# Row selection on TensorE for the first two sub-blocks of a dynamic convolution with a squared-ReLU FFN

## The chip, the core and the metric

The kernel runs on one core of a Trainium2 chip. The metric is the device time of one execution in microseconds, as the median over several runs. The engines named below are TensorE (PE, matmul; PEld is its weight load), VectorE (DVE), ScalarE (ACT), GpSimd (POOL) and SyncE (SP). SP only issues DMAs here, and POOL mostly does.

## The reference

Two layers follow each other over 8 sequences of 4096 rows of 192 features.

The first is a dynamic convolution. Each row has, for each of 8 heads, 7 raw weights. They go through a softmax over the 7 taps, and the row's output is the weighted sum of the row itself and the 6 rows before it, head by head (24 features each):

```python
w = np.exp(weight_gen - max); w = w / (sum + 1e-09)            # (B, S, 8, 7)
x_unf = x_pad[:, np.arange(S)[:, None] + np.arange(7)[None, :], :]
out = np.einsum('bshk,bskhg->bshg', w, x_unf.reshape(B, S, 7, 8, 24))
```

The second is a feed-forward layer on all 32768 rows: `h = max(x @ w_in, 0)`, then `(h * h) @ w_out`, with 2048 hidden features.

## The kernel before, in words

**Sub-blocks and blocks.** The rows are cut into 64 sub-blocks of 512 (`TB`). `BLOCKS` holds two blocks of one sub-block each, then blocks of two sub-blocks. In a block of two sub-blocks, the upper 64 rows of the 128-row array work for one of them and the lower 64 for the other ("half"). The first two blocks cut their one sub-block in two halves of 256 rows in the same way.

**Softmax and rows.** The softmax of sequence 0 is done in four parts of 1024 rows, 8 rows per partition: `exp` on ScalarE (line 250), `total` (257), `recip` (264) and `scale` (272) on VectorE. `scale` writes the weights into `v_first`, whose row order is that of the partitions: partition p holds rows 8p to 8p+7. The convolution needs them one row per partition, in five overlapping tiles of 128 rows per sub-block, `wr`. Before, `wr_load_sbuf` (363) moves them there by DMAs from SBUF to SBUF. The first part feeds sub-blocks 0 and 1; sub-block 0's five DMAs go over SP and POOL, those of sub-block 1 over POOL.

**Band and convolution.** `st_band` (381) multiplies the `wr` tile by `mask` and so spreads the seven weights of each row onto a band matrix `bd`. `st_conv` (487) multiplies x with the band: TensorE matmuls with 32 output features each, on one of four column strips of the array, into `yp`. A copy (503) brings `yp` to `y` in half precision.

**Units and quarters.** A unit, `st_unit` (518), makes 1024 columns of hidden values `h` in PSUM: for each half, the 192 features are contracted in three slots of 64. ScalarE takes the ReLU into `t1` (532), VectorE squares it into `g` (536). `st_mm2` (560) is the second matrix product; one call handles 8 of the 16 hidden chunks for a quarter of 256 rows, and the letter M in the plans stands for one such call. `o_sum` (574, 576) and `o_store` (581) end a quarter after its second call. Since the two halves sit in different rows of the array, `w_i` is kept twice: part 0 as loaded and part 1 with the upper and lower 64 partitions swapped. The swap of half q=0 of `w_i` is done by TensorE with the matrix `swap` (149) and two copies (153), the swap of q=1 by two DMAs (`cross_w_in`, 141).

**Order.** It is written out by hand. Each engine takes its instructions in the order in which the program names them. Before the first unit stands a start-up section with `spin` matmuls (624), which compute nothing that is used. Then each block has a plan: a string whose letters are steps. u is a unit, M a call of `st_mm2`, C the convolution of the next block, E and S the exp and the rest of a softmax part, B the bands of a sub-block, L the load of a part, X the cast of x. M always takes the next call that is due (`quarters`).

**Buffers.** The PSUM pool `ps_h` has three buffers in rotation, shared by `h` and `yp`; `ps_o` has the two banks `o0` and `o1`. `w_out` is loaded by POOL in four pieces (`load_w_out`, 194) after the copy `gate` (657) has seen x of sub-block 1.

Of the kernel before, what the change touches and what calls it, by code (L numbers as in the profile page):

```python
# [9 lines left out]
def kernel(  # L10
# [26 lines left out]
    nc = tc.nc  # L37
    f32 = mybir.dt.float32
# [17 lines left out]
    BLOCKS = [(0, 1), (1, 1)] + [(n, 2) for n in range(2, NSUB, 2)]  # L56
    NBLK = len(BLOCKS)
    NF = Dff // P

# [9 lines left out]
    starts = [BASE + STEP * i for i in range(NT)]  # L69
    bounds = [0, 104, 208, 312, 416, TB]  # L70

    AluOp = mybir.AluOpType
# [24 lines left out]
    mask = const.tile([P, P, 2], f16, name="mask")  # L97
    swap = const.tile([P, P], f16, name="swap")
    FIRST = 8
    PARTS = {0: (8, 8, 8, 8), 1: (8, 8, 16), 2: (16, 16)}  # L100
    v_big = const.tile([P, R + 2 * HALO, HP, SL, 2], f16, name="v_big")
# [3 lines left out]

    def half_swap():

        nc.gpsimd.memset(swap, 0.0)
        for base in (RT, -RT):
            nc.gpsimd.affine_select(  # L110
                out=swap, in_=swap, pattern=[[-1, P]], compare_op=AluOp.not_equal,
                fill=1.0, base=base, channel_multiplier=1,
            )

# [24 lines left out]
    def cross_w_in(q):  # L139
        for r0, r1 in ((0, RT), (RT, 0)):  # L140
            nc.sync.dma_start(out=w_i[r0 : r0 + RT, q, 1], in_=w_i[r1 : r1 + RT, q, 0])

    def cross_w_in_by_pe(q):
        n = NQ + NQ // 2
        for a in range(0, n, 2 * TB):
            b = min(a + 2 * TB, n)
            pt = ps_h.tile([P, 2 * TB], f32, name="pt", tag="h")
            for c in range(a, b, TB):
                nc.tensor.matmul(
                    out=pt[:, c - a : c - a + TB], lhsT=swap, rhs=w_i[:, q, 0, c : c + TB],  # L150
                    start=True, stop=True,
                )
            nc.scalar.copy(out=w_i[:, q, 1, a:b], in_=pt[:, 0 : b - a])

# [145 lines left out]

    x_t, wr_t, bd_t, yp_t, y_t, g_t, gp_t, t1_t, o_t, o_sb_t = ({} for _ in range(10))

# [51 lines left out]
    def wr_load_sbuf(j, parts, order, engines):  # L354
# [3 lines left out]
        for i in order:  # L358
            t0 = max(j % NBB * TB + tile_start(j, i), 0)
            for s in parts:  # L360
                a, b = max(t0, s.t0), min(t0 + P, s.t0 + P * s.r)
                if a < b:
# [6 lines left out]
                    n += 1  # L369

    def st_band(j, tiles):


        if j not in bd_t:
            bd_t[j] = p_bd.tile([P, H * NT * STEP], f16, name="bd")
        i = tiles[0]
        lo = STEP * i
        shift = 0 if i == 0 and j % NBB == 0 else lo - tile_start(j, i)
        n = min(STEP, P - shift)
        shape = (P, HP * len(tiles), n // SL, 2 * SL)  # L380
        nc.vector.tensor_tensor(  # L381
            out=bd_t[j][:, H * lo : H * (lo + len(tiles) * n)].rearrange(
                "p (g m c) -> p g m c", g=shape[1], c=2 * SL
            ),
            in0=wr_t[j][:, i : tiles[-1] + 1]
            .rearrange("p t g c -> p (t g) c")
            .unsqueeze(2)
            .broadcast_to(shape),
            in1=mask[:, shift : shift + n]
            .rearrange("p (m c) e -> p m (c e)", c=SL)  # L390
            .unsqueeze(1)
            .broadcast_to(shape),
            op=AluOp.mult,
        )
# [7 lines left out]
    def conv_pieces(j):  # L402
# [5 lines left out]
        for half in (0, 1):  # L408
# [4 lines left out]
            ])  # L413
        if n == 2:
            for k in range(NK):
                for later in (True, False):
                    for pair in zip(*halves):
                        for s, i, half, a, b, base in pair:
                            for q in (2 * k, 2 * k + 1):
                                yield later, s, i, q, half, a, b, base  # L420
        else:
            for pair in zip(*halves):
                for later in (True, False):
                    for k in range(NK):
                        for s, i, half, a, b, base in pair:
                            for q in (2 * k, 2 * k + 1):
                                yield later, s, i, q, half, a, b, base

# [37 lines left out]
    def st_conv(j):  # L466

        if j >= FIRST_SPREAD:
            return st_conv_spread(j)
        n = BLOCKS[j][1]  # L470
        th = n * TB // 2
        per = 1024 // th
        y = p_y.tile([P, NK, TB], f16, name="y")
        y_t[j] = y
        yps = [
            ps_h.tile([P, 2 * TB], f32, name="yp", tag="h") for _ in range(-(-NK // per))
        ]
        for later, s, i, q, half, a, b, base in conv_pieces(j):
# [6 lines left out]
            k = q // 2  # L485
            col = th * (k % per) - base
            nc.tensor.matmul(  # L487
                out=yps[k // per][p0 : p0 + m, col + a : col + b],
                lhsT=x_t[s][:, i, 32 * q : 32 * q + m],
# [6 lines left out]
        for n, yp in enumerate(yps):  # L496
            k0, k1 = n * per, min((n + 1) * per, NK)

            copies = ((k0, k1, nc.scalar.copy),)
            if j == 0:  # L500
                copies = ((0, 2, nc.scalar.copy), (2, NK, nc.vector.tensor_copy))
            for a, b, copy in copies:
                copy(  # L503
                    out=y[:, a:b, 0:th],
                    in_=yp[:, (a - k0) * th : (b - k0) * th].rearrange("p (k c) -> p k c", c=th),
                )

    def st_unit(j, u):

        th = BLOCKS[j][1] * TB // 2  # L510
        per = TB // th
        w = w_p if j >= FIRST_SPREAD else w_i
        h = ps_h.tile([P, 2, TB], f32, name="h", tag="h")
        for jj in range(per):
            for slot in range(NK):
                for half, r0 in enumerate((0, RT)):
                    k = slot ^ half if slot < 2 else slot
                    nc.tensor.matmul(  # L518
                        out=h[:, half, jj * th : (jj + 1) * th],
                        lhsT=w_in_chunk(w, u * per + jj, slot, half),  # L520
                        rhs=y_t[j][r0 : r0 + RT, k, 0:th],
                        start=(jj == 0 and slot == 0), stop=(slot == NK - 1),
                        skip_group_check=True,
                        tile_position=(r0, 0),
                    )
# [22 lines left out]
    def st_mm2(j, qt, fcs, ccs, o):  # L548


        th = BLOCKS[j][1] * TB // 2
        per = TB // th
        half, off = divmod(qt * QT, th)
        for fc in fcs:
            g = g_t[(j, fc // per)][:, half, fc % per * th + off :]
            for cc in ccs:
# [38 lines left out]
    with nc.allow_low_precision("fp16 matmul pipeline"), tc.manual_schedule():  # L595
# [19 lines left out]
        gate = const.tile([P, 1], f32, name="gate")  # L615
        nc.vector.memset(warm, 0.0)
        for v in v_first:
            nc.vector.memset(v, 0.0)
# [3 lines left out]
        def spin(n):  # L622
# [3 lines left out]
        s0, s1, s2 = parts[:3]  # L626
        spin(25)
        half_swap()
        band_mask()
# [4 lines left out]
            for q in (0, 1)  # L634
        ]
        load_w_in(w_st[0], 0, nc.sync)
        x_load_f32(0)
        load_w_in(w_st[1], 1, nc.sync)
# [3 lines left out]
        s0.scale(0, s0.rh, nc.vector)  # L642
        nc.scalar.copy(out=w_i[:, 0, 0], in_=w_st[0])
        wr_load_sbuf(0, [s0], (0, 2, 1, 4, 3), (nc.sync, nc.gpsimd))
        wr_load_sbuf(1, [s0], range(NT), (nc.gpsimd,))
        x_cast(0, nc.scalar.copy)
        cross_w_in_by_pe(0)
        spin(14)
        x_load_f32(1)
        nc.scalar.copy(out=w_i[:, 1, 0], in_=w_st[1])  # L650
        cross_w_in(1)
        s1.load(nc.sync)
        for i in (0, 2, 1, 3, 4):
            st_band(0, (i,))
        st_conv(0)

        nc.gpsimd.tensor_copy(out=gate, in_=x_st[1][:, 0:1])
        for q in range(4):
# [9 lines left out]
        plans = {  # L668
            0: "B1 X1 u u u E1 S1 u C u u u u",
            1: "L3 u u B2 M E2 B3 u M E2 u u S2 u M u C u S2 M",  # L670
            2: "L4 u u u E3 M u u u M B4 u u u u M B5 S3 u u u u M u E3 C u",
            3: "L5 L6 M S3 u u u M u u u u M u M B6 E4 u u u M M B7 u u u E4 M u M C S4 u",
        }
# [94 lines left out]
        def quarters():  # L768

            for j in range(NBLK - 1):  # L770
                for qt in range(2 * BLOCKS[j][1]):
                    o = new_o(ps_o, 1, qt % 2) if j < 2 else new_o(ps_o)
                    st_mm2(j, qt, FCS[0], (0, 1), o)
                    yield
                    st_mm2(j, qt, FCS[1], (0, 1), o)
                    o_sum(j, qt, (0, 1), o)
                    if qt % 2:
                        o_store(j, qt - 1, range(4), nc.sync)
                    yield

        mm2 = quarters()
        for j in range(NBLK):
            if j + 2 < NBLK:
                load_rows(j + 2)
            u = 0
            for step in plans[j].split():
# [23 lines left out]
                elif kind == "L":  # L810
                    parts[n].load(nc.sync)
                elif kind == "X":
                    x_cast(n, nc.vector.tensor_copy)
# [47 lines left out]
```

The softmax here doesn't subtract the row's maximum and nothing guards it: scores larger than these inputs give would overflow.

## Time and profile before

| | us |
|---|---|
| median of 6 runs | 734.82 (734.37 to 737.21) |
| profiled execution | 734.35 |
| its span | 732.6 |
| TensorE busy in the span | 724.8 (99%) |
| VectorE busy | 627.3 (86%) |
| ScalarE busy | 613.6 (84%) |
| start of the first unit | 15.49 |
| start of the first ReLU | 16.60 |
| start of the convolution of block 2 | 33.33 |
| start of block 2's first unit | 37.05 |

The span runs from the first to the last instruction on the core, and all start times below count from its beginning. TensorE's busy time contains pipelined waits, so 99% says that TensorE always has something to do, not that it works at its peak. The granted TensorE clock is 1.00 in all slices.

### The profile page before, as it was taken

How to read it: one execution, taken by the hardware profiler on the slowest of the kernel's cores; microseconds unless marked ns; L12 is line 12 of the kernel's file. 1: busy time of each engine (PE TensorE's matmuls, PEld its weight loads, DVE VectorE, ACT ScalarE, POOL GpSimd, SP SyncE). 2: the span in 40 equal slices, each digit the busy share in tenths (PEclk: the TensorE clock that was granted, in tenths of full speed). 3: DMA queues.
4: the chain of work that ended last, by engine and by line, in shares of the span. 5: the costliest groups of instructions: out<-in, count | busy, mean ns of one | idle time of the engine just before them, and what ended most of it. 6: DMA issues, size and time to landing. Idle time of an engine off the chain costs nothing.

```text
span 732.6 us, 31124 instructions
## 1 busy us (share of the span) xinstructions
PE 724.8 (99%) x14106; PEld 528.9 (72%) x14106; DVE 627.3 (86%) x856; ACT 613.6 (84%) x724; POOL 99.8 (14%) x148
## 2 busy tenths in 40 slices
PE   8999999999999999999999999999999999999998
PEld 4757777777777777777777777777777777777777
DVE  5999898998898988888988888988889988778753
ACT  5998888988888888888888888888888888888883
POOL 7312222320001100011000010010100110001000
PEclk9999999999999999999999999999999999999999
DMA  8745444783545452455333554334544315444012
GB/s 222 119 96 123 81 71 105 144 160 115 99 66 128 95 90 60 78 125 119 62 73 69 117 123 83 61 71 120 104 87 86 57 49 120 67 87 78 30 45 67
DMA packets 126544, 68.71 MB, mean 94 GB/s; under 512 B 85193, under 2 KB 122636, under 8 KB 125900
## 3 DMA queue, kind: packets, MB, share of 16 engines
q1 hardware_dynamic: 80908, 48.12, 22.9%
q0 software_dynamic: 45360, 18.50, 21.7%
q8 instruction: 110, 1.80, 1.0%
q14 instruction: 22, 0.18, 0.1%
q10 hardware_dynamic: 144, 0.10, 0.0%
HBM read 50.18 MB, written 28.70 MB: 108 GB/s over the span
## 4 chain that ended last, share of the span: by engine, by line
PE 96%; ACT 1%; DMA 1%; DVE 1%; issue 0%; DVEq 0%
PE o L560 47%; PE h L518 45%; PE yp L450 4%; PE yp L487 1%; ACT t L532 1%; DMA wr<-v_first 0%; DMA wg<-in_weight_gen_dram 0%; DVE bd L381 0%; ACT ex L250 0%; DVE v_first L272 0%; ACT y L503 0%; DVE ssum L257 0%; DVE rcp L264 0%; DVE y L503 0%; ACT o_sb L574 0%
## 5 line engine op out<-in xcount | busy, mean ns | idle before, releaser
L532 ACT ACTIVATE t<-h 128x1024 f16<-128x1024 f32 x512 | 496.4, 1026 | 60.0 <-PE h L518 59.7
L560 PEld LDWEIGHTS <-g 64*128 64x128 f16 (+1 forms) x8032 | 342.7, 94 | 55.7 <-issue 2.5
L560 PE MATMUL o<-w_o,g 64*128 64x192 f16 (+1 forms) x8032 | 379.1, 243 | 0.0
L536 DVE TENSOR_TENSOR g<-t 128x2048 f16<-128x2048 f16 (+1 forms) x309 | 309.3, 1037 | 28.1 <-ACT t L532 27.7
L518 PE MATMUL h<-y,w_p 64*128 64x512 f16 x2400 | 291.7, 376 | 0.0
L518 PEld LDWEIGHTS <-w_p 64*128 64x128 f16 x2400 | 113.8, 94 | 94.8
L381 DVE TENSOR_TENSOR bd<-wr,mask 128x4160 f16<-128x4160 f16 (+3 forms) x89 | 149.4, 1703 | 3.5 <-DMA wr<-v_first 3.5
L576 DVE TENSOR_TENSOR o_sb<-o,o_sb 128x384 f32<-128x384 f32 x123 | 68.4, 556 | 60.8 <-ACT o_sb L574 59.9
L333 POOL DMA_DIRECT2D xt<-in_x_dram x62 | 51.8, 839 | 421.6 <-PE yp L450 362.6
L574 ACT COPY o_sb<-o 128x384 f32<-128x384 f32 x129 | 61.5, 477 | 46.8 <-PE o L560 46.0
L518 PE MATMUL h<-y,w_i 64*128 64x512 f16 (+1 forms) x768 | 82.2, 350 | 1.7 <-ACT t L532 0.7
L518 PEld LDWEIGHTS <-w_i 64*128 64x128 f16 x768 | 36.8, 94 | 28.1 <-issue 3.9
L450 PEld LDWEIGHTS <-xt 128*32 128x32 f16 x2000 | 24.5, 95 | 10.6 <-issue 10.6
L272 DVE TENSOR_TENSOR v_big<-ex,rcp 128x112 f16<-128x112 f32 (+5 forms) x180 | 29.8, 236 | 1.9 <-DMA vd<-v_big 0.9
L460 DVE CAST y<-yp 128x1024 f16<-128x1024 f32 x25 | 30.4, 1218 | 0.0
L450 PE MATMUL yp<-bd,xt 128*32 128x104 f16 (+1 forms) x2000 | 28.3, 210 | 0.0
L250 ACT ACTIVATE ex<-wg 128x560 f32<-128x560 f32 (+4 forms) x38 | 25.9, 683 | 1.8 <-DMA wg<-in_weight_gen_dram 1.8
L257 DVE TENSOR_REDUCE ssum<-ex 128x80 f32<-128x560 f32 (+4 forms) x38 | 25.3, 666 | 2.3 <-ACT ex L250 2.3
L460 ACT CAST y<-yp 128x1024 f16<-128x1024 f32 x25 | 25.2, 1007 | 0.0
L264 DVE RECIPROCAL rcp<-ssum 128x80 f32<-128x80 f32 (+4 forms) x38 | 22.8, 601 | 1.3
L323 POOL DMA_DIRECT2D xt<-in_x_dram x7 | 3.9, 555 | 124.6 <-PE yp L450 109.7
L363 POOL DMA_DIRECT2D wr<-v_first x31 | 16.9, 563 | 16.0 <-DVE v_first L272 15.8
(34 smaller groups left out, 95.1 us busy)
## 6 DMA issues: line engine op xcount, KB each, us to landing
out_dram<-o_sb SPq DMA_DIRECT2D x63, 384.0 KB
xt<-in_x_dram POOLq DMA_DIRECT2D x42, 240.0 KB, 5.2
wg<-in_weight_gen_dram SPq DMA_DIRECT2D x4, 1064.0 KB
xt<-in_x_dram POOLq DMA_DIRECT2D x20, 192.0 KB, 4.7
wr<-vd SPq DMA_DIRECT2D x38, 80.0 KB
vd<-v_big SPq DMA_DIRECT2D x5, 512.0 KB
y<-y SPq DMA_DIRECT2D x100, 24.0 KB
wg<-in_weight_gen_dram SPq DMA_DIRECT2D x5, 392.0 KB
```

What stands on the lines that cost most here:

```text
L250: nc.scalar.activation(out=self.ex[:, lo:hi].rearrange("p r g k e -> p (r g) k e"), in_=self.wg[:, lo:hi].rearrange("p r (g e) k -> p (r g ...
L272: eng.tensor_tensor(out=bass.AP(tensor=v.tensor, offset=v.offset + lo * H * SL + lo % SL * 2 + g * SL * 2, ap=[list(v.ap[0]), [H * SL + 2, ...
L333: eng.dma_start(out=dst[:, first:last], in_=ap)
L381: nc.vector.tensor_tensor(out=bd_t[j][:, H * lo : H * (lo + len(tiles) * n)].rearrange("p (g m c) -> p g m c", g=shape[1], c=2 * SL), in0= ...
L450: nc.tensor.matmul(out=yp[p0 : p0 + 32, k - k0, a:b], lhsT=x_t[s][:, i, c0 : c0 + 32], rhs=bd[:, head // 2, e, 0 : b - a], start=True, sto ...
L460: copy(out=y[:, k0 : k0 + 2], in_=yp)
L518: nc.tensor.matmul(out=h[:, half, jj * th : (jj + 1) * th], lhsT=w_in_chunk(w, u * per + jj, slot, half), rhs=y_t[j][r0 : r0 + RT, k, 0:th ...
L532: nc.scalar.activation(out=t1[:, e], in_=h, func=ActF.Relu)
L536: nc.vector.tensor_tensor(out=g[:, a : e + 1], in0=t1[:, a : e + 1], in1=t1[:, a : e + 1], op=AluOp.mult)
L560: nc.tensor.matmul(out=oo[:, cc * Dm : (cc + 1) * Dm], lhsT=g[r0 : r0 + n, cc * P : (cc + 1) * P], rhs=w_o[r0 : r0 + n, fc, :], start=(fc ...
L574: nc.scalar.copy(out=o_sb, in_=o[0][:, c])
L576: nc.vector.tensor_tensor(out=o_sb, in0=o[1][:, c], in1=o_sb, op=AluOp.add)
```

## The change

1. **Rows.** For sub-blocks 0 and 1, TensorE picks the rows. `sel` holds a shifted selection pattern, so that a window of 128 of its columns takes every row of a residue r to its place. Eight accumulating matmuls of 64 columns (r from 0 to 7) make one `wr` tile in PSUM (`pr`), and ScalarE copies it to `wr`. The five tiles of sub-block 0 come first; those of sub-block 1 stand between the five tiles of sub-block 0's convolution. The row DMAs of these two sub-blocks go. `swap` and its selects go; `sel` is cleared by VectorE and filled by one affine select on POOL ahead of `mask`.
2. **First two blocks.** The convolution puts features 0 to 127 on all four column strips, as block k=0 over all 512 columns, and features 128 to 191 twice, on both halves, as k=1. A unit then makes two chunks of hidden features for 512 rows: two matmuls over 128 rows of the array and two over 64 rows, with a change of order from unit to unit. It needs part 0 of `w_i` only.
3. **`w_i`.** Half q=0 is cast by ScalarE between the row copies, half q=1 by VectorE (step W). Both swapped parts are made by DMAs on SP, issued at the start of block 1 (q=0) and of block 2 (q=1).
4. **Order.** x of sub-block 0 is loaded ahead of `w_i`. Block 0's plan makes C before S1, with one unit more before it, and has an M before its last two units; block 3's plan has one M fewer, its first. The calls of the first two blocks come first half of both quarters, then second half of both. 21 spins instead of 25 at the start, and none of the 14 later ones.

The core of the diff:

```diff
-    def half_swap():
...
+    def row_select():
+        nc.gpsimd.affine_select(
+            out=sel, in_=sel, pattern=[[-1, NSEL]], compare_op=AluOp.not_equal,
+            fill=1.0, base=FIRST - 1, channel_multiplier=FIRST,
+        )
...
+    def select_rows(j, s, tiles, places):
...
+            for r in range(s.r):
+                c = a + FIRST - 1 - r
+                nc.tensor.matmul(
+                    out=pr, lhsT=sel[:, c : c + P],
+                    rhs=s.v[:, HALO + r].rearrange("p g c e -> p (g c e)"),
+                    start=(r == 0), stop=(r == s.r - 1),
+                )
...
+    def st_conv_first(j, between=None):
...
+        places = [(q, 32 * q, 0) for q in range(4)]
+        places += [(q, r0 + 32 * (q - 4), 1) for r0 in (0, RT) for q in (4, 5)]
+        for i in ROW_ORDER:
...
+            for later in (True, False):
+                for q, p0, k in places:
...
+            if between:
+                between(i)
+        if j == 0:
+            nc.scalar.copy(out=y[:, 0], in_=yp[:, 0])
+            nc.vector.tensor_copy(out=y[:, 1], in_=yp[:, 1])
...
+    def first_unit(u, h, y):
+        q, f = divmod(u, NF // WQ // 2)
+        both = [
+            (h[:, n], w_i[:, q, 0, (f + n * NF // WQ // 2) * P :][:, 0:P], y[:, 0], 0)
+            for n in (0, 1)
+        ]
+        upper = [
+            (h[:, n], w_i[r0 : r0 + RT, q, 0, NQ + f * P :][:, 0:P], y[r0 : r0 + RT, 1], r0)
+            for n, r0 in enumerate((0, RT))
+        ]
+        pairs = (upper, both) if u % 2 else (both, upper)
...
+        nc.vector.memset(sel, 0.0)
...
-        spin(25)
-        half_swap()
+        spin(21)
+        row_select()
...
+        x_load_f32(0)
         load_w_in(w_st[0], 0, nc.sync)
-        x_load_f32(0)
         load_w_in(w_st[1], 1, nc.sync)
...
-        nc.scalar.copy(out=w_i[:, 0, 0], in_=w_st[0])
-        wr_load_sbuf(0, [s0], (0, 2, 1, 4, 3), (nc.sync, nc.gpsimd))
-        wr_load_sbuf(1, [s0], range(NT), (nc.gpsimd,))
         x_cast(0, nc.scalar.copy)
-        cross_w_in_by_pe(0)
-        spin(14)
         x_load_f32(1)
-        nc.scalar.copy(out=w_i[:, 1, 0], in_=w_st[1])
-        cross_w_in(1)
         s1.load(nc.sync)
+        select_rows(0, s0, ROW_ORDER, (o1, ring, ring, ring, o0))
+        copy_rows(0, ROW_ORDER)
...
+        def next_rows(i):
+            n = ROW_ORDER.index(i)
+            select_rows(1, s0, (i,), ((o1, ring, ring, o0, o1)[n],))
+            if n < 2:
+                copy_rows(1, (i,))
+            if n == 1:
+                nc.scalar.copy(out=w_i[:, 0, 0], in_=w_st[0])
+
+        st_conv_first(0, next_rows)
+        copy_rows(1, ROW_ORDER[2:])
...
-            0: "B1 X1 u u u E1 S1 u C u u u u",
+            0: "B1 X1 W u u u u E1 C S1 u u M u u",
...
-            3: "L5 L6 M S3 u u u M u u u u M u M B6 E4 u u u M M B7 u u u E4 M u M C S4 u",
+            3: "L5 L6 S3 u u u M u u u u M u M B6 E4 u u u M M B7 u u u E4 M u M C S4 u",
...
+            if 1 <= j <= WQ:
+                cross_w_in(j - 1)
...
+                elif kind == "W":
+                    nc.vector.tensor_copy(out=w_i[:, 1, 0], in_=w_st[1])
```

Blocks 1 and 2 keep their plans ("L3 u u B2 M E2 B3 u M E2 u u S2 u M u C u S2 M" and "L4 u u u E3 M u u u M B4 u u u u M B5 S3 u u u u M u E3 C u").

## The prediction, made before the changed kernel was run

> **What bounds it now.** I read the PE waits first, then the chain of work in order of time, then DVE, SP and PE in order of time. After 15 us TensorE waits for other engines only three times, and after 100 us never:
>
> ```profile
> PE h L518 <- ACT t L532: 0.7, 1, 0.7
> PE h L518 <- ACT y L503: 0.7, 1, 0.7
> PE yp L487 <- DVE xt L347: 0.3, 1, 0.3
> ```
>
> So a microsecond won or lost on TensorE before block 4 arrives whole at the end, and the rest is a fixed tail. The chain shows what the change touches (start, length, work):
>
> ```profile
> 6.76 1.47 DVE v_first L272 x8
> 8.25 3.38 DMA wr<-v_first
> 11.72 2.61 DVE bd L381 x5
> 14.38 0.45 PE yp L487 x16
> 14.86 0.59 ACT y L503
> 15.47 0.44 DVE y L503
> 15.95 0.63 PE h L518 x8
> 16.60 2.25 ACT t L532 x3
> ```
>
> The row transfer takes 3.38 us, and the first ReLU starts at 16.60. From there to 28.8 ScalarE runs without a gap at 0.91 us per ReLU, while TensorE has holes: the ACT-bound stretch. VectorE is nearly gapless from 15.8 to 41.7, and two lines of its order and two of SP's will matter:
>
> ```profile
> 15.81 2.35 DVE L381 TENSOR_TENSOR bd<-wr,mask 128x3328 f16<-128x3328 f16 x2
> 39.16 0.72 DVE L272 TENSOR_TENSOR v_first<-ex,rcp 128x84 f16<-128x84 f32 x4
> 12.93 1.16 SPq L141 DMA_DIRECT2D w_i<-w_i  x2
> 39.90 3.67 SPq L363 DMA_DIRECT2D wr<-v_first  x5
> ```
>
> The profiled execution took 734.35 us, span 732.6 and 1.7 around it; the median is 734.82, 0.5 above. I sum against 734.35 and shift the result by 0.5.
>
> **The head.** The load, exp, total, reciprocal and the products stay and end at 8.22. The new memset of `sel` (1031 columns; 640 words take 0.59 us, so at most 1.1) lies in VectorE's 2.31 us idle before `ssum`. The affine select over 1031 columns is not in the trace: 128 columns take 0.29, 256 of the mask 1.24. That bounds it between 1.0 (memset-like rate) and 5.0 us; I take 1 to 2.3, as the 128-column row has the same one-dimensional pattern. The mask is then done by 6.4 to 7.7, before the first band at 8.9; only 5.0 makes it late, by about 1.4.
>
> One tile of rows is 8 matmuls of 64 columns with full 128x128 weights. No row has that. In M the 128x128 pairs start 82.5 ns apart for 192 columns (80 of streaming, 2.5 more): the weight load is hidden. In the conv, matmuls on one column strip start 25 ns apart for 48 columns, 27 for 56, 47 for 104. So 64 columns lie between 27 and 82.5 ns; I take 30, as the first two weight loads of an M start 15 ns apart. A tile: 0.24 us. On one rule I decide against the page: the Trainium skill, TensorE: Matmul & The Clock Gate, Back-to-back issue gap, gives 81 ns for a stream of weight load and matmul at 128 columns, 28 above streaming. M's 2.5 above streaming disagrees; by the page a tile would take about 0.44 and the sum below would end near no change.
>
> First tile: six matmuls remain after the last product, 0.15, then 0.24 from a last conv matmul's start to the ScalarE copy that needs it: 8.64. The copy of 64 columns, from 477 ns at 384 and 1023 at 1024, is 0.20. Band 0 starts at 8.9 and ends at 9.5; five bands 0.50 apart end at 11.5. TensorE finishes the five tiles at 9.4, and then alternates: conv tile (16 matmuls in 4 rounds of 47 ns) 0.19, rows for sub-block 1 0.24, and twice a change of array layout. The layout's price: sixteen M matmuls are 1.32 us, but from M's start at 25.46 to the next unit's at 26.88 it takes 1.43, so 0.1. Together 0.62 per tile, four times: the fifth conv tile starts at 12.0 and its copy at 12.4. ScalarE's cast of `w_i` (1.47, after two copies at 10.9) ends just then. The y copies: 0.59 on ScalarE, 0.70 on VectorE (256 columns took 0.43, 1024 1.22). A first unit: two full-array matmuls at 0.216, a layout change, two concurrent halves: 0.74. First ReLU at about 14.2: 2.4 us sooner.
>
> The 128-feature form costs nothing on its own: 3x512 column times per unit, as 6x256 before; its layout change is hidden in the ACT-bound stretch (0.74 against 0.91), and later replaces the one that units beside an M paid. The swap by TensorE, its two copies (1.49) and 14 spins lay before the first unit, on no later path. Four spins fewer at the start leave a hole of 0.9 us before 8.25; before, one of 1.0 was passed with the granted clock at 1.00.
>
> **Block 0 and 1.** VectorE's next band starts at 13.3 instead of 15.81, after the three last row copies on ScalarE. Its work is the same plus the cast W: 960 columns took 0.69, so 1536 are 0.97 net. Thus the bands that conv 2 needs end at 13.3 + (32.62 - 15.81) + 0.97 = 31.1 instead of 32.62, and TensorE gets to conv 2 then too: 31.2 instead of 33.33. By then one M more is done: M in block 0 starts at 18.8, after the squares of four units, and ends at 20.4, in time for unit 6. One M with its layout changes is 1.43 + 0.1. At conv 2 the gain stands at 2.1 + 1.5 = 3.6. On POOL, w_o is gated by x of sub-block 1, now loaded as soon as its predecessor is cast: gate at 12.0 by 0.3 MB per us (2.47 MB moved by 10.0), w_o's second quarter at about 19.0, just about M.
>
> **What eats it.** The swap of half q=1 of `w_i`, which was issued on SP at 12.93, moves to the start of block 2. SP's queue places it behind five row transfers that wait for the second S2. That ends at 13.3 + (39.87 - 15.81) + 0.97 = 38.3. Five issues of 0.64 take 3.2, the two swap issues start at 41.6 and 42.2. They landed 2.8 and 3.05 us after issue before; the range is 2.0 to 3.5 by the landings of rows and bulk loads. So the second half is there at 45.05. Unit 8 of block 2 needs it in its second pair of matmuls: before at 45.51, now at 43.4 (31.2 + 12.2). TensorE waits 1.65, with everything behind it. Behind the swaps on SP stand only a load and a store with time to spare. Swap q=0 is issued at 26 and needed at 35: hidden.
>
> Second, block 3 no longer opens with an M. It covered the y copies of conv 3, which end at 55.45 and 55.93 while the last unit ends at 55.16. Four of the six matmuls of the next unit need only the first copy: start 0.32 late, and the last pair 0.05 more: 0.4 lost.
>
> Sum: at unit 8, 45.51 - 45.05 = 0.46, plus the M 1.52, minus 0.38: **1.6 us sooner**. 734.35 - 1.6 = 732.75; as a median 733.2.
>
> **Rivals.**
> - *The swap is hidden.* If it lands by 43.4, the gain is 3.6 minus about 0.4: 731.6. For it: POOL's row transfers land 2.0 to 2.6 after issue. Against: it must land within 1.2 of its issue, or the rows before it must wait less. Partial relief is in the forecast's range.
> - *Slower: the row selection is weight-bound.* Nine tiles lie before the fifth conv tile: 72 pairs. At 82.5 ns they cost 72 x 52.5 = 3.8 us more: 1.6 - 3.8, 737.0. No change is reached at 52 ns, 0.2% slower at 73. For it: the weights start at every column of `sel`, also odd ones, where all weights of before start at multiples of 8; and no row has so few columns at full width. Against: the 15 ns between loads.
> - *w_o comes late.* Were the gate not sooner than 14.56, the second quarter would be there at 22.8 as before, M in block 0 would hold units 6 and 7 in TensorE's order for 3.5 us, and ScalarE would run dry: the M's 1.5 and more go, 735.1. Against: x of sub-block 1 need not wait for row transfers now.
> - The selection, earlier M and swaps are all there in the order of instructions, so the change does what it says.
>
> **The numbers.** Forecast 0.58, its own range 732.0 to 734.6 (landing 2.0 to 3.5; pairs 27 to 41 ns, the upper end from the later M's of 32 half-array pairs in 1.32 us); hidden swap 0.17; weight-bound 0.15; late w_o 0.10. A measurement tells 0.2%, 1.5 us, from no change; the forecast stands just across it. Faster: 0.58 x 0.53 + 0.17 = 0.48. Within: 0.26 of the forecast, 0.08 of late w_o, 0.01: 0.35. Slower: 0.14 of weight-bound and 0.03 of the others: 0.17. The range 731.0 to 736.8 leaves out about half of the weight-bound case and the best of the hidden one.
>
> **What would show it.** First ReLU at 14.2 (17.9 if weight-bound); tiles of eight matmuls in 0.24; TensorE gapless in the ACT-bound stretch where M stands; conv 2 at 31.2; then a TensorE wait at a unit of block 2, ended by DMA `w_i`, of 1.65, and a short one after conv 3. No wait for `w_i` and the hidden swap is right. A first ReLU after 16, or a wait for `mask` or `w_o` in the first 20 us, and the sum is wrong in its head.

## The result and the profile after

The changed kernel is slower: 739.15 us (median of 21 executions, 736.50 to 740.94) against 735.11 for the kernel before, measured with it (43 executions); ratio 1.0047, interval 1.0038 to 1.0057, so 0.5% and clear of the noise. The forecast was 733.2, its range 731.0 to 736.8. The profiled execution took 740.23, with a span of 738.5.

The head came out as forecast. Chain of work in order of time (start, length, work), changed kernel:

```profile
8.27 0.35 PE pr L369 x6
...
8.64 0.22 ACT wr L378
...
8.96 0.61 DVE bd L392
...
9.70 0.38 PE yp L448 x13
10.08 0.34 PE pr L369 x8
...
11.21 1.48 ACT w_i L713
...
12.70 0.59 ACT y L460
...
13.31 0.69 DVE y L461
```

Where 3.38 us of row transfer stood, there is one tile of selection, a copy of 0.22 and the first band at 8.96. The first ReLU starts at 14.49, 2.1 sooner than before. What follows is the loss. The waits after 14 us (engine, tile, line, and behind the arrow the releaser, that is what the wait ended with; then us in total, times, longest):

```profile
DVE bd L392 <- DMA wr<-v_first: 2.8, 2, 1.4
...
PE h L565 <- DMA w_i<-w_i: 2.7, 2, 2.3
...
PE o L614 <- DMA w_o<-in_moe_w_out_dram: 1.7, 1, 1.7
```

Three waits for transfers that the kernel before did not have there. The first in time is `w_out` at M in block 0. POOL in order of time, with what ended the idle time in brackets:

```profile
15.28 0.56 POOL L718 COPY gate<-x_st 128x1 f32<-128x1 f32 x1 [6.61 <-DMA x_st<-in_x_dram]
15.80 3.48 POOL L183 DMA_DIRECT2D w_o<-in_moe_w_out_dram  x4
```

The gate opened at 15.28 (before 14.56), `w_out` was issued behind it, and the M that started at 19.81 took 3.12 us from first to last matmul instead of 1.24. VectorE in order of time shows the second; the first line is the kernel before, the others are the changed one:

```profile
28.03 4.59 DVE L381 TENSOR_TENSOR bd<-wr,mask 128x4160 f16<-128x4160 f16 x3
...
29.90 4.60 DVE L392 TENSOR_TENSOR bd<-wr,mask 128x4160 f16<-128x4160 f16 x3 [1.43 <-DMA wr<-v_first]
...
41.51 0.72 DVE L261 TENSOR_TENSOR v_first<-ex,rcp 128x84 f16<-128x84 f32 x4
```

And SP in order of time the third (the span of a line runs from its first issue to its last):

```profile
34.38 11.07 SPq L352 DMA_DIRECT2D wr<-v_first  x6
45.50 1.95 SPq L142 DMA_DIRECT2D w_i<-w_i  x2
```

The band of sub-block 2 starts at 29.90 (before 28.03) after waiting 1.43 for rows, so the second S2 ends at 42.23 (before 39.87), its rows are issued until 45.5, and the swap of half q=1 goes out at 45.50. TensorE was ready to load these weights at 46.34 and had the last of them at 49.82. The windows around this wait (busy time of PE, PEld, DVE, ACT and POOL with counts; then granted TensorE clock, DMA share, GB/s):

```profile
46.00:48.00 2.00, 0.71 (x8) 0.10 (x2) 0.65 (x2) 1.84 (x2) 0.00 (x0) 1.00 0.46 88
48.00:50.00 2.00, 0.57 (x3) 0.23 (x5) 2.00 (x2) 0.00 (x0) 0.00 (x0) 0.84 0.88 234
50.00:51.00 1.00, 1.00 (x6) 0.30 (x4) 1.00 (x3) 0.11 (x1) 0.00 (x0) 0.50 0.49 194
51.00:52.00 1.00, 1.00 (x5) 0.14 (x1) 0.29 (x2) 0.91 (x1) 0.00 (x0) 0.50 0.00 0
52.00:53.00 1.00, 1.00 (x9) 0.91 (x9) 0.63 (x1) 0.83 (x1) 0.00 (x0) 0.61 0.00 0
```

TensorE is busy for 1.28 of 4 us, and then the granted clock is 0.50 for some 3.4 us (that is what 0.84, 0.50, 0.50 and 0.61 in these windows add up to): the work that the wait held up also runs at half speed. The group of units 6 to 9 takes 6.47 us from its first to its last matmul, instead of 2.39, the M behind it 1.58 instead of 1.25.

Starts of the convolutions in the profiled executions (us), and medians:

| kernel | conv 2 | conv 3 | conv 4 | conv 6 | median |
|---|---|---|---|---|---|
| before | 33.33 | 53.00 | 75.53 | 120.61 | 735.11 |
| changed | 34.06 | 58.48 | 80.30 | 125.87 | 739.15 |
| both swaps in block 1 | 34.10 | 53.55 | 75.46 | 121.24 | 735.32 |
| the same, `w_out` sooner | 31.98 | 52.67 | 76.23 | 121.65 | 735.52 |
| spins in the wait | 34.60 | 56.85 | 78.66 | 123.92 | 737.41 |

At convolutions 2 and 3 the changed kernels have done one M (1.5 us) more than the kernel before, from convolution 4 on the same number. Most of the loss of the changed kernel arises between convolutions 2 and 3, where the swap is waited for: 4.75 us more than in the kernel before. The medians come from different sessions and chips, in which the kernel before itself had 735.11 (with the changed kernel), 734.59 (experiments 1 to 4) and 734.83 (5 to 8), so a difference of two of them is good to about half a microsecond.

### The profile page after: what moved, and what is told of

Its sections match the earlier page's. It is cut to its first block, busy times and chain, and to the rows that moved or that the text cites. A ratio compares the mean times of both kernels' runs of the same rounds, so it can differ in the third digit from the quotient of the medians.

```text
span 738.5 us, 31011 instructions
## 1 busy us (share of the span) xinstructions
PE 727.4 (98%) x14053; PEld 529.0 (72%) x14053; DVE 630.1 (85%) x858; ACT 613.1 (83%) x731; POOL 97.0 (13%) x139
## 4 chain that ended last, share of the span: by engine, by line
PE 92%; DVE 3%; DMA 1%; ACT 1%; issue 1%; SPq 1%; POOL 0%; DVEq 0%
PE o L614 45%; PE h L565 43%; PE yp L486 4%; DVE g L583 1%; PE yp L520 1%; DVE bd L392 1%; DVE v_first L261 1%; DMA wr<-v_first 1%; DMA wg<-in_weight_gen_dram 0%; DMA w_i<-w_i 0%; DVE ssum L246 0%; DVE rcp L253 0%; SPq L352 0%; POOL wr L352 0%; ACT w_i L713 0%
## 5 line engine op out<-in xcount | busy, mean ns | idle before, releaser
L565 PE MATMUL h<-y,w_i 64*128 64x512 f16 x576 | 72.2, 380 | 2.9 <-DMA w_i<-w_i 2.7
L565 PEld LDWEIGHTS <-w_i 64*128 64x128 f16 x576 | 30.8, 94 | 25.9 <-DMA w_i<-w_i 3.5
L352 POOL DMA_DIRECT2D wr<-v_first x24 | 13.0, 567 | 13.1 <-DVE v_first L261 8.6
```

The costliest lines, as they stand in the source:

```text
L565: nc.tensor.matmul(out=h[:, half], lhsT=w_in_chunk(w, u, slot, half), rhs=y_t[j][r0 : r0 + RT, k], start=(slot == 0), stop=(slot == NK - 1 ...
```

## The experiments

The theory after the result, A: the swap of `w_i` behind the rows on SP's queue makes the loss. Its rival, B: the loss is made in the first 30 us by `w_out` and the rows. Below, a ratio is always to the kernel before on the same chip, with its interval.

**1. Both swaps issued in block 1.**

```diff
-            if 1 <= j <= WQ:
-                cross_w_in(j - 1)
+            if j == 1:
+                for q in range(WQ):
+                    cross_w_in(q)
```

> Only edit to the changed kernel: both swaps of w_i are issued on SP at the start of block 1, so q=1 no longer stands behind the row transfers of the second S2. Theory A (the swap behind the rows is the main loss): its issue moves from 45.5 to about 29, it lands by 33, TensorE's wait of 2.3 to 3.7 us at unit 8 of block 2 goes and so does the slower clock after it; 734.5 to 736.0, level with before. Theory B (the loss is made in the first 30 us, by w_out and the rows coming late): TensorE only waits elsewhere, 738 to 739.

Measured: 735.32, ratio 1.0012 (1.0003 to 1.0020). A, as expected. The wait for `w_i` is gone, the clock is 1.00 throughout, and of the waits of TensorE for transfers this one remains:

```profile
PE o L614 <- DMA w_o<-in_moe_w_out_dram: 1.5, 1, 1.5
```

The place of the swap costs 739.15 - 735.32 = 3.8 us, or 3.3 if each is taken against the kernel before of its own session. But the kernel does not become faster than before.

**2. `w_out` released by `w_i` instead of x of sub-block 1.**

```diff
-        nc.gpsimd.tensor_copy(out=gate, in_=x_st[1][:, 0:1])
+        nc.gpsimd.tensor_copy(out=gate, in_=w_st[0][:, 0:1])
```

> Only edit to the changed kernel: the gate of the w_out load reads the first half of w_in instead of x of sub-block 1, so w_out starts some 4 us sooner. Theory A: M in block 0 no longer waits 1.7 us for w_out, but the swap still comes behind S2 and the row issues, which move by at most 1 us; 738 to 739.2. Theory B: 736.5 to 737.5, the whole 1.7 us and the ScalarE idle after it come back.

Measured: 739.0, ratio 1.0057 (1.0043 to 1.0072): A again. M in block 0 no longer waits (1.24 us) and convolution 2 is reached at 32.51, 1.55 sooner than in the changed kernel. The swap is issued at 45.56, where it was, so TensorE only waits longer. It was not the softmax that held it there: the rows of the second S2 start on SP at 41.16, 1.1 sooner than in the changed kernel (42.26), but the fifth of these issues takes 1.76 us, where the four before it take about 0.6:

```profile
43.75 1.76 SPq L352 DMA_DIRECT2D wr<-v_first  x1
```

What held this issue no run shows. In the changed kernel it was the first issue of the swap itself that took long (1.31). TensorE's wait for `w_i` in this kernel:

```profile
PE h L565 <- DMA w_i<-w_i: 3.0, 2, 2.8
```

The clock stays low longer, too, as the windows show (granted clock third from the right):

```profile
48.00:50.00 2.00, 1.43 (x5) 0.39 (x7) 2.00 (x3) 0.00 (x0) 0.00 (x0) 0.51 0.83 239
50.00:52.00 2.00, 2.00 (x11) 0.86 (x8) 0.80 (x2) 1.50 (x2) 0.00 (x0) 0.50 0.03 13
52.00:54.00 2.00, 2.00 (x14) 1.70 (x12) 1.42 (x2) 0.55 (x1) 0.00 (x0) 0.50 0.00 0
```

**3. Both edits.**

> Both edits together. Theory A: the wait for the swap is gone, and what the head loses now counts, so the gate is worth 1 to 2 us here that it is not worth alone; 733 to 734.5, faster than before. Theory B: 736.5 to 737.5, the same as with the gate alone.

Measured: 735.52, ratio 1.0010 (1.0001 to 1.0018). That is 1 us above A's number and 1 us below B's: with the swap out of the way, `w_out` on time is worth nothing either. VectorE in order of time tells why:

```profile
28.76 4.59 DVE L392 TENSOR_TENSOR bd<-wr,mask 128x4160 f16<-128x4160 f16 x3 [1.61 <-issue]
...
46.46 2.33 DVE L392 TENSOR_TENSOR bd<-wr,mask 128x4160 f16<-128x4160 f16 x1 [1.26 <-DMA wr<-v_first]
```

TensorE gets to convolution 2 at 31.98, but VectorE has stood 1.61 us before the band of sub-block 2; the convolution takes 2.59 us instead of 1.40. The profile names no releaser for this wait; in the changed kernel and in experiment 12 it names the rows at the same place. Convolution 3 stalls 0.67; there the rows are named. In block 3 VectorE is so late that an M waits for the sum of its output:

```profile
PE o L614 <- DVE o_sb L630: 0.9, 1, 0.9
```

**4. Block 0 without its M, block 3 with its first M back.**

```diff
-            0: "B1 X1 W u u u u E1 C S1 u u M u u",
+            0: "B1 X1 W u u u u E1 C S1 u u u u",
...
-            3: "L5 L6 S3 u u u M
+            3: "L5 L6 M S3 u u u M
```

> Only edit to the changed kernel: the M goes from block 0 back to the start of block 3; all else stays, the swap too. Theory A: TensorE arrives sooner at unit 8 of block 2 and waits longer for the same swap, with one M less done; the swap comes up to 1 us sooner, the M costs 1.5 and covers 0.4 in block 3: 739 to 740. Theory B (M that waits for w_out is what costs): 736.5 to 737.5.

Measured: 741.41, ratio 1.0086 (1.0073 to 1.0099), above both expectations. The swap is issued at 45.54 once more, while TensorE is at unit 8 earlier; its group takes 6.62 us. That is 2.3 us above the changed kernel (2.8 against the kernel before of each session). The early M is worth more than its 1.5 us here, since it is work done in front of the wait; what makes up the rest was not taken apart.

**5. Matmuls in the wait.** Does the clock cost something by itself?

```diff
+                    if (j, u) == (2, 8):
+                        hp = ps_h.tile([P, TB], f32, name="hp", tag="h")
+                        for i in range(12):
+                            nc.tensor.matmul(out=hp, lhsT=warm[:, 0:P], rhs=warm, start=True, stop=True)
                     st_unit(j, u)
```

> The changed kernel with twelve matmuls of 512 columns on spare data ahead of unit 8 of block 2, the unit whose second half waits about 4 us for the swapped half of w_i. They write a buffer that nothing reads and take 12 x 0.213 = 2.6 us, which lies inside the wait. Theory 1: the fall of the granted clock to 0.72 after that wait is TensorE standing still for 4 us, and costs the stretched M (1.581 for 1.249) and part of the units after it. Then the hole shrinks to about 1.5 us, the clock stays at 1.00 and the time is 738.0 to 738.8, against about 739.2. Rival: the fall has nothing to do with the idle stretch, or it costs nothing by itself because the wait for w_i sets the end: 739.0 to 739.6 with the clock again at about 0.997.

Measured: 737.41, ratio 1.0035 (1.0022 to 1.0048): faster than the changed kernel although TensorE has 2.6 us more to do. The windows of the same stretch:

```profile
48.00:50.00 2.00, 2.00 (x13) 0.77 (x13) 1.67 (x3) 0.07 (x1) 0.00 (x0) 1.00 0.82 244
50.00:51.00 1.00, 1.00 (x11) 0.44 (x8) 0.00 (x0) 0.78 (x1) 0.00 (x0) 1.00 0.00 0
```

The clock stays at 1.00. The gain, 1.7 us, is more than expected (0.4 to 1.2), and not all of it need be the clock: in the profile of this kernel the swap was issued 1.0 us sooner than in that of the changed kernel (45.50), because the band of sub-block 2 did not wait for its rows, although the edit comes only behind it:

```profile
44.52 2.35 SPq L142 DMA_DIRECT2D w_i<-w_i  x2
```

The clock alone can be read from the two profiles: from the second pair of matmuls of unit 8 to the next group of units TensorE took 4.00 us at half clock (49.82 to 53.82) and 2.61 at full clock (49.58 to 52.19), so some 1.4 us. A price of this size fits the changed kernel's own executions: the 8 with a mean clock of 0.999 or more took 736.5 to 738.1 (median 737.4), the 13 with 0.995 to 0.998 took 738.7 to 740.9 (median 739.9). Why the clock falls in some executions only is open; that the rows come sooner in some of them, as in this profile, would be one reason.

**6. Short spins.** In the kernel of experiment 1, TensorE stops for 0.63 us in an M of block 5, at 101.2, and no releaser is named. The window there, of that kernel and of the kernel before:

```profile
101.00:101.90 0.90, 0.43 (x11) 0.20 (x9) 0.87 (x6) 0.90 (x2) 0.90 (x2) 1.00 1.00 305
```
```profile
101.00:101.90 0.90, 0.90 (x22) 0.76 (x19) 0.86 (x5) 0.90 (x2) 0.90 (x2) 1.00 1.08 291
```

The first line is the kernel of experiment 1, the second the kernel before: same work, same transfers, but 11 matmuls for 22. The edit puts 63 matmuls more in front, in the same time:

```diff
-            for i in range(n):
-                nc.tensor.matmul(out=wp, lhsT=warm[:, 0:P], rhs=warm, start=True, stop=True)
+            for i in range(4 * n):
+                nc.tensor.matmul(
+                    out=wp[:, 0:P], lhsT=warm[:, 0:P], rhs=warm[:, 0:P], start=True, stop=True
+                )
```

> The kernel with both swaps in block 1 (735.32), with 84 spins of 128 columns in place of the 21 of 512 at the start: the same TensorE time ahead of the first row selection, but 63 matmuls and 63 weight loads more in TensorE's stream. In every version of the changed kernel TensorE stopped in the middle of an M, ahead of its 1759th matmul, for 0.28 to 0.80 us (at 101.2 in the kernel with both swaps early, where the x loads of a later block move 300 GB/s), and the trace names no releaser. Theory 1: what stops there is tied to a place in the stream of instructions, which comes in by DMA and collides with the x loads. Then the stop moves 63 matmuls back in the work, into convolution 5, where the DMA engines are nearly idle: no hole at 101.2, and 734.5 to 735.0. Rival: the M waits for VectorE or for data at this point of the work: the hole stays in the same M, now ahead of the 1822nd matmul, and the time is 735.3.

Measured: 735.96, ratio 1.0018 (1.0008 to 1.0028); the time of neither theory. The stop at 101 is gone, as theory 1 said, but there is a new one of 2.0 us at 12.4, in convolution 0 ahead of TensorE's 224th matmul, again without a releaser. The stop does not belong to the work of that M, then. The wait of this kernel:

```profile
PE yp L448 <- issue: 1.8, 1, 1.8
```

And two of its windows, with half the clock behind the stop:

```profile
12.00:14.00 2.00, 0.58 (x19) 0.39 (x11) 0.00 (x0) 0.99 (x1) 0.00 (x0) 1.00 1.08 229
...
16.00:17.00 1.00, 1.00 (x5) 0.13 (x4) 1.00 (x2) 0.00 (x0) 1.00 (x3) 0.50 0.09 26
```

The packets of the DMA queues in the traces say more. The queue that the profile calls `q8 instruction` carries 110 packets of 16 KB in each kernel, about one for every 256 of TensorE's matmuls and weight loads. In all eleven kernels with the stop ahead of the 1759th matmul, this matmul starts 1.30 to 1.47 us after the 13th of these packets has landed; the 224th matmul of experiment 6 starts 1.33 after the first has (11.67 to 13.06). In experiment 5, where the 1759th matmul stands 12 places earlier in the work, it too starts 1.34 after the 13th packet, 0.08 late. So these stops end with the arrival of instructions.

**7. x of sub-block 3 behind the rows** (on the kernel of experiment 1).

```diff
-                    if j == 0:
-                        x_load(3)
-                    elif j + 2 < NBLK:
+                    if 0 < j and j + 2 < NBLK:
...
                     soft(parts[n])
+                    if n == 1:
+                        x_load(3)
```

> The kernel with both swaps in block 1 (735.32), with the load of x of sub-block 3 issued on POOL behind the rows that the first softmax part of 1024 rows leaves for block 2, not ahead of them. Theory 1: these rows came late (up to 30.7, VectorE's band of sub-block 2 waited 0.8) because x and w_out were being moved at the same time. With x out of the way the band does not wait, convolution 2 starts at 33.2 instead of 34.1 and the time is 734.4 to 734.8. Rival: the rows are late by their issues (ten at about 0.6 us on two queues, after the end of the scale at 23.9) and by their own transfer, and x takes no part: band and convolution stay where they are, 735.2 to 735.6, or x is then late itself and convolution 2 starts later than 34.1.

Measured: 734.91, ratio 1.0002 (0.9993 to 1.0012), between the two ranges. VectorE's band of sub-block 2 starts at 28.33 without a wait, as theory 1 said, though one profile does not prove it: in that of experiment 5 it did not wait either, with x ahead of the rows. Convolution 2 starts at 34.01 all the same, against theory 1. It hangs on ScalarE, which stood 2.0 us at the M that waits for `w_out`. So two chains end at convolution 2 close to each other: `w_out`, M, ReLU; and softmax, rows, band.

**8. The softmax part for block 2 earlier** (experiments 3 and 7, and):

```diff
-            0: "B1 X1 W u u u u E1 C S1 u u M u u",
+            0: "B1 X1 W u E1 S1 u u u C u u u u M",
...
-            3: "L5 L6 S3 u u u M u u u u M u M B6 E4 u u u M M B7
+            3: "L5 L6 M S3 u u u M u u u u M u M B6 E4 u u u M B7
```

> Both swaps in block 1, w_out released by w_i, x of sub-block 3 behind the rows, block 0 with the softmax part for block 2 after one unit instead of five and its M last, and block 3 with its first M back (one of the two that stand together later goes instead). Theory 1: the earlier version with the first two edits stayed at 735.5 because what the head gained was lost again to late rows (VectorE waited 1.6 and 1.3 us for them, convolutions 2 and 3 stalled 1.2 and 0.65) and to block 3 (0.4 at the copies of y, 1.1 in an M that waited for o). Here the scale ends at about 21.8 instead of 23.5, no band waits, convolution 2 starts at 31 to 32 without a stall and block 3 has its cover: 731.5 to 733.5, below both kernels. Rival: VectorE has no room; what the softmax takes sooner the squares get later, TensorE waits for g or ScalarE for t in block 0, and the time stays at 735 to 736.

Measured: 736.49, ratio 1.0025 (1.0014 to 1.0035): the rival, and 0.5 above its range. The band of sub-block 2 starts at 27.73 without a wait, but the M back in block 3 waits 1.3 us for squares just made, and the exp of block 0 now waits for its load:

```profile
ACT ex L239 <- DMA wg<-in_weight_gen_dram: 0.9, 1, 0.9
```

**9. The last M of block 2 behind convolution 3** (on experiment 7).

```diff
-            2: "L4 u u u E3 M u u u M B4 u u u u M B5 S3 u u u u M u E3 C u",
+            2: "L4 u u u E3 M u u u M B4 u u u u M B5 S3 u u u u u E3 C M u",
```

> The kernel with both swaps in block 1 and x of sub-block 3 behind the rows (734.91), with the last M of block 2's plan moved behind the convolution of block 3. Theory 1: block 3 now opens while ScalarE still copies y of convolution 3, since the changed kernel has no M there; the unit group after it lost 0.33 at one matmul. With an M and one unit between convolution and the first unit of block 3 the copies are covered and the end comes 0.3 to 0.4 sooner: 734.4 to 734.7. Rival: the M moved is missed where it stood (ScalarE or VectorE fall behind without it, or o is not free behind the convolution) and the time is 734.9 to 735.5.

Measured: 734.76, ratio 0.9999 (0.9989 to 1.0009). The 0.33 us at the copies of y is gone; a unit of block 2 that had the M in front of it now starts 0.25 late. Within the measurement, nothing.

**10. The softmax part after two units, with M behind convolution 3** (on experiment 8, with block 2's plan of experiment 9 and block 3's of the changed kernel).

```diff
-            0: "B1 X1 W u E1 S1 u u u C u u u u M",
+            0: "B1 X1 W u u E1 S1 u u C u u u M u",
```

> Both swaps in block 1, w_out released by w_i, x of sub-block 3 behind the rows, the softmax part for block 2 after two units of block 0 (after one unit its exp waited 0.95 us for its load), block 0's M behind its seventh unit, block 3 as in the changed kernel and the last M of block 2 behind convolution 3. Theory 1: in the kernel with this part after one unit ScalarE lost 0.95 at the load and convolution 1 came 1.8 us later for it, and block 3's first M waited 1.3 for squares just made; both go here, rows come by 28, convolution 2 starts at 32 to 33 with no stall and with one M more behind it than before: 732.5 to 734.3, below the kernel before. Rival: the chain of softmax, squares and M on VectorE allows no order that gains: the M waits for squares, ScalarE for TensorE, and the time is 735 to 736.5.

Measured: 735.36, ratio 1.0000 (0.9991 to 1.0009): the rival. The exp still waits 0.8 for its load, the M 0.6 for squares, and convolution 2 starts at 34.13.

**11. W on POOL** (on experiment 10; the cast takes the gate's place).

```diff
-        nc.gpsimd.tensor_copy(out=gate, in_=w_st[0][:, 0:1])
+        nc.gpsimd.tensor_copy(out=w_i[:, 1, 0], in_=w_st[1])
```

> The kernel of the softmax part after two units, with the cast of the second half of w_i (step W) on POOL in front of the loads of w_out instead of on VectorE. Theory 1: VectorE is what block 0 and 1 wait for; it is freed of 0.95 to 1.16 us before the softmax part, so rows, bands and convolution 2 come up to 1 us sooner, and w_out, issued after the cast, still lands before the M behind the seventh unit: 0.5 to 1.0 below the kernel with W on VectorE. Rival: TensorE is held by ScalarE's units there, or the cast on POOL takes over 4 us and makes w_out or the fifth unit late: the same as with W on VectorE or up to 2 above.

Measured: 735.59, ratio 1.0002 (0.9993 to 1.0011): the rival. POOL takes 2.97 us for the cast, `w_out` is issued from 17.47 on, and VectorE's two bands beside the cast take 3.62 instead of 2.35.

**12. Experiment 3 with x of sub-block 3 behind the rows** (the edit of experiment 7).

> Both swaps in block 1, w_out released by w_i, block 0 in the order of the changed kernel, and x of sub-block 3 behind the rows. Without the last edit it took 735.52: M in block 0 had no wait and convolution 2 was reached at 31.98, but VectorE waited 1.6 us for rows before the band of sub-block 2, and the convolution stalled 1.2. Theory 1: x of sub-block 3 shares the DMA engines with these rows; behind them it frees 0.8 us, as it did in the kernel with both swaps early (band of sub-block 2 at 28.33 for 29.31). Then the stall falls to 0.4 or less, everything after comes about 0.8 sooner and the time is 734.3 to 734.9. Rival: what is won in the head is lost at the next place that waits for rows or squares (the band of sub-block 4, an M of block 3), and the time stays at 735.2 to 735.8.

Measured: 735.68, ratio 1.0007 (0.9997 to 1.0018): the rival. VectorE in order of time:

```profile
28.59 4.59 DVE L392 TENSOR_TENSOR bd<-wr,mask 128x4160 f16<-128x4160 f16 x3 [1.36 <-DMA wr<-v_first]
```

The wait for the rows is 1.36; the band starts 0.17 sooner than in experiment 3, not 0.8. So in this kernel x of sub-block 3 is not what holds the rows. What does (the ten issues, or the other loads) stays open. No version tried is faster than the kernel before; the best, experiment 9, is level with it.

## Why the prediction was wrong

The forecast was 5.95 us too low. The runs divide that as follows (medians): half clock 739.15 - 737.41 = 1.7, from experiment 5; the wait itself 737.41 - 735.32 = 2.1, from experiment 1, where 1.65 was in the sum; and 735.32 - 731.55 = 3.8 that experiment 1 still has (731.55 is the forecast without its swap wait). 1.7 + 2.1 + 3.8 - 1.65 is the 5.95. With each median taken against the kernel before of its session the three are 1.5, 1.9 and 4.0. So the larger part of the error lies in the gain without any swap wait, and the smaller in the swap.

**What held.** The affine select of `sel` took 1.04 (1 to 2.3 expected). Eight selection matmuls start within 0.20 to 0.22, 29 to 31 ns a pair, where I took 30. So the weight-bound rival falls. The rule that I had set aside (the Trainium skill, TensorE: Matmul & The Clock Gate, Back-to-back issue gap: 81 ns for a weight load and a matmul at 128 columns) does not show at 128 columns either: the 84 spins of experiment 6, each with a load of its weights (always the same), start 107 ns apart up to 5 us and 56 ns apart from then on. First copy 8.64, first band 8.96, fifth conv tile 12.28, first ReLU 14.49 (forecast 8.64, 8.9, 12.0, 14.2). Block 3's loss at the copies of y was there: 0.44 for 0.38. The mechanism of the swap was right, too, and only its size was off: a wait for `w_i` in unit 8 of block 2, ended by a DMA 2.97 us after the second issue at 46.85 (forecast 2.85).

**The step that failed first** is in the head: "gate at 12.0 by 0.3 MB per us". x of sub-block 1 was issued at 7.40 and 7.78, as its predecessor was cast, but landed at 15.23. The pace of 0.3 MB per us was an average over the loads before; it does not say in which order queues that share the engines are served. So "w_o's second quarter at about 19.0, just about M" became a wait of 1.7 us, and ScalarE stood for 2.1: the rival with the chance of 0.10, in part. The range ended at 736.8 because I let the rivals come one at a time.

**From there the sum carried the error on.** "The bands that conv 2 needs end at 31.1" became 34.5: VectorE reached band 2 about 2 us later than forecast, and then waited 1.43 more for rows; that rows could be late I had not priced at all. Of the 2 us, 0.6 were there from the start (VectorE's copy of `y` waited for ScalarE's, and its next band began at 13.92 for 13.3), and 1.0 is the late `w_out`: in experiment 2 VectorE reached band 2 at 27.44, not 28.47. "That ends at 38.3" became 42.23, and the swap's issue 45.50 instead of 41.6. The swap was placed behind a chain whose end I took as a single number, with a range only for the landing. A late `w_out` alone does not explain it, since in experiment 2 the swap went out at 45.56 all the same, behind an issue of 1.76. TensorE came to unit 8 later as well (its first pair started at 46.33, so the second was due at about 46.55, for 43.4), which hid part of the shift: where the head was sooner, the wait was longer, as experiment 2 showed.

**The term that was missing** is the clock. I had noted that a hole of 1.0 passes with the clock at 1.00, and did not ask at what length it no longer does; the wait of 3.5 had a price beyond its length. The Trainium skill has such a price (TensorE: Matmul & The Clock Gate, Part 1: The HAM clock gate: the clock falls to half after an idle window of about 3.4 us and needs a busy one of that length to come back). The trace agrees with the half clock and with its length, some 3.4 us. It differs in that the stretch before the fall was not idle: the fall came after 4 us with 1.28 of work in them, and in experiment 6 after a stop of 2.0 us and short ones behind it.

**The step that cost most** is "At conv 2 the gain stands at 2.1 + 1.5 = 3.6". Without any swap wait, experiment 1 stands at 0.7 there (the 1.5 us of one M more, less 34.10 - 33.33). The 2.1 us of the head are lost to the M's wait for `w_out`. Where that is mended, in experiment 3, convolution 2 stalls 1.2 in place of it, and some 2.4 go between convolutions 3 and 4: convolution 3 starts 0.33 sooner than in the kernel before with one M more done, convolution 4 starts 0.70 later with the same number. In experiment 1 block 3 takes 0.7, of which 0.44 are at the copies of y, and the stop in block 5 takes 0.6. That is why a hidden swap gives 735.3 and not the 731.6 of the rival.

## What to carry to other kernels

When a transfer moves to another place in a queue, price its issue as a chain with a range at every link, and ask what happens when every link is late at once. A gain at the head of a kernel is only worth what the next transfer leaves of it: find the second chain that ends at the same place, since mending one alone gave nothing here, and the orders that mended both (experiments 8 and 10) met a third. And this wait of 3.5 us on TensorE cost more than its length: half the clock behind it stretched the work by 1.4 us, and the kernel that filled it with idle matmuls was 1.7 us faster.

## What the runs showed of the hardware

- Towards the end of 4 us in which TensorE worked 1.28, the granted clock fell to 0.50, for some 3.4 us. It stretched the work by 1.4 us in the profile; the kernel without the fall was 1.7 us faster in the median.
- TensorE stopped ahead of its 1759th matmul in all eleven kernels whose stream of instructions was as long as the changed kernel's up to there, for 0.20 to 0.80 us, and hardly or not at all in the two with 12 or 63 matmuls more in front (0.08 and 0). Experiment 6, which took this stop away, got one of 2.0 us ahead of the 224th. Each of these matmuls started 1.30 to 1.47 us after a packet of 16 KB had landed on the queue `q8 instruction`, so the supply of instructions ends the stop. What makes a packet late is open: at the 1759th matmul it took 0.95 to 1.44 us, against 0.88 for the shortest, and that the transfers of 300 GB/s beside it matter was not tested.
- The cast of 1536 columns took 0.95 to 1.16 us on VectorE and 2.97 on POOL, and VectorE's two bands beside the cast on POOL took 3.62 us instead of 2.35.
